# Top-k attention and MLP on one core: q/k loads ten steps later, and value copies moved behind the step's exponents

## The chip, the core and the metric

The kernel runs on one core of a Trainium2 chip. The metric is the device time of one execution in microseconds (us), here as a median over several runs. The engines are named as the profile names them: PE is TensorE (PEld its weight loads), DVE is VectorE, ACT is ScalarE, POOL is GpSimd, and SP is SyncE, which here issues every transfer. SPq is the SyncE queue's own work of issuing.

## The reference

Sparse attention is followed by a two-layer MLP. For 8 batches of 8 heads, 576 tokens and a head size of 64:

```python
scores = scale * np.matmul(q, k.transpose(0, 1, 3, 2))
kth = np.partition(scores, -top_k, axis=-1)[..., -top_k:-top_k + 1]   # top_k = 32
scores = np.where(scores >= kth, scores, -1000000000.0)
attn = np.exp(scores - np.max(scores, axis=-1, keepdims=True))
attn = attn / (np.sum(attn, axis=-1, keepdims=True) + 1e-09)
x = np.matmul(attn, v)                  # then heads side by side: 4608 tokens x 512
h = x @ w_in                            # 512 -> 2048
out = np.maximum(0.01 * h, h) @ w_out   # 2048 -> 512
```

So each row of scores keeps its 32 largest entries, and everything else gets a weight of zero.

## The kernel before

**Units and steps.** Two heads that lie side by side form a pair; there are 32 pairs, four to a batch. A unit is 128 query rows of one pair with both its heads (or the left-over 64 rows of two pairs), so a batch has 18 units, and there are 144 in all. The main loop walks over steps `s`, one unit a step. The order of every engine's instructions is the order in which this loop writes them (`manual_schedule`); no scheduler moves them. In step `s`:

- VectorE searches the 32 largest entries of unit `s` (`top_k`: four rounds of MAX8 at L249 and MATCH_REPLACE8 at L252, from the halves that L244 makes). A round is a `slot()`.
- GpSimd masks unit `s - 1` (`mask`, L262 and L263).
- ScalarE takes the exponents of unit `s - 1` (`exponents`, L266, first head in mid-step, second head at the end) and writes their sums (`sums`, `ze`, L271).
- Unit `s - 2` is normalized: reciprocals on VectorE (`rz`, L275), the product on ScalarE (L278). Then its weights are transposed: ScalarE splits the words into 16-bit halves (`split`, L287), SyncE writes them to DRAM (`apart`, L288) and reads them back with a transposing DMA (`wT`, L290). Units 15, 23 and 31 (`HURRIED`) are transposed on TensorE instead (L300), and ScalarE copies the result from PSUM (L306).
- Every second step TensorE computes the scores of the two units that begin two and three steps later (`scores`, L214), and ScalarE copies them out of PSUM (L221).
- Every second step TensorE weighs the values of two older units (`weigh_values`, L327), and ScalarE copies the result to `x` (`keep_values`, L341). For units 0 to 13 that stands in the middle of a step (`MIDDLE`), four steps after the later unit; afterwards at the end of a step (`END`), three steps after it, or two for a hurried unit.
- Between these, `mlp_steps` puts pieces of the MLP of token chunks that are ready: the first layer at L378 (at L352 for the first two chunks, with transposes at L362), its activation at L384, the second layer at L390, the copy and the store at L397 and L398. A chunk is ready when the values of all its units are in `x`.

**What sets the order around the change.** [...] A copy `x<-wide` on ScalarE waits for TensorE's L327, and whatever the step wrote behind it on ScalarE waits as well. A transfer issued by SyncE waits in the same way ahead of the writes and transposes that follow.

**Loads.** q and k of a pair (288 KB each, `load_qk`, L162 and L163) have eight places: five in the pool `loads`, three in the pool `raws`, which held the weights at first. v of a pair (320 KB, `load_v`, L168) has five. At the end of each step `load_more(s)` starts the loads whose place is free: those of q and k from the step on in which the scores of the place's last unit have been written, since `last[pair] - 2 <= s`; those of v four steps after that unit's own step. Two pairs come free in the same step in even batches.

**Before the loop** the weights of the MLP come as 64-bit words and are put together in single precision (L102 to L149), until about 75 us. At the end, when no unit is left, the rest of the MLP runs alone.

Of the kernel before, what the change touches and what calls it, by code (L numbers as in the profile page):

```python
# [19 lines left out]
def kernel(  # L20
# [35 lines left out]
    LOADED, LOADED_V = 5, 5  # L56
# [38 lines left out]
    def load_weights(n):  # L95
        if n >= NPIECE:
            return
        if not AS_WORDS:
            nc.sync.dma_start(piece(n), weights[n])
            return  # L100
        raw_of[n] = raws.tile([P, WCH, 4], U16, name="raw")
        nc.sync.dma_start(raw_of[n].rearrange("p n w -> p (n w)"), weights[n])  # L102
# [50 lines left out]
    qk_of, v_of = {}, {}  # L153

    def load_qk(pi):
        if pi % (LOADED + 3) < LOADED:
            qt = loads.tile([P, S], F32, name="qt")
            kt = loads.tile([P, S], F32, name="kt")
        else:
            raw = raws.tile([P, WCH, 4], U16, name="raw").rearrange("p n w -> p (n w)").bitcast(F32)  # L160
            qt, kt = raw[:, 0:S], raw[:, S:2 * S]
        nc.sync.dma_start(qt, qT[pi])  # L162
        nc.sync.dma_start(kt, kT[pi])  # L163
        qk_of[pi] = qt, kt

    def load_v(pi):
        v_of[pi] = loads.tile([P, NKC, 2, D], F32, name="vt", bufs=LOADED_V)
        nc.sync.dma_start(v_of[pi], vk[pi])  # L168
# [54 lines left out]
    def first_scores(u):  # L223

        ps = [ps_sc.tile([P, 2, 512], F32, name="wide", bufs=2) for i in range(2)]
        for half in range(2):
            for i, pi, side, r0 in u.parts:
                qt, kt = qk_of[pi]
                d = slice(side * D, (side + 1) * D)
                nc.tensor.matmul(ps[i][:, half, 0:HS], qt[d, u.q0:u.q0 + P],  # L230
                                 kt[d, half * HS:(half + 1) * HS], start=True, stop=True)
        u.both = work.tile([P, 2, S], F32, name="s_sb", bufs=5)
        u.s = [u.both[:, i, :] for i in range(2)]
        for i in range(2):
            nc.scalar.copy(u.s[i].rearrange("p (h n) -> p h n", h=2), ps[i][:, :, 0:HS])
# [33 lines left out]
    def sums(u):  # L269
        u.ze = small.tile([P, 2], F32, name="ze")  # L270
        nc.scalar.activation(u.ze, u.z, AF.Copy, bias=1e-9, scale=1.0)  # L271

    def reciprocals(u):
        u.rz = small.tile([P, 2], F32, name="rz")
        nc.vector.reciprocal(u.rz, u.ze)  # L275

    def normalize(u, i):
        nc.scalar.activation(u.s[i], u.s[i], AF.Copy, bias=0.0, scale=u.rz[:, i:i + 1])  # L278
# [33 lines left out]
    def x_at(token):  # L312

        c = 0
        while token >= CHUNKS[c]:
            token -= CHUNKS[c]
            c += 1
        return c, token

    def weigh_values(u, po):  # L320
        n = u.rows
        po = po.rearrange("p (o n) -> p o n", n=n)
        for o, (pi, r0, r1) in enumerate(u.outs):
            vt = v_of[pi]
            for c in range(NKC):
                for side, r in ((0, r0), (1, r1)):
                    nc.tensor.matmul(  # L327
                        po[side * D:(side + 1) * D, o, :],
                        vt[:, c, side, :],
                        u.wT[:, c + side * NKC if c + 1 < NKC else c, r:r + n],  # L330
                        start=(c == 0), stop=(c == NKC - 1),
                    )

    def keep_values(u, po):
        n = u.rows
        po = po.rearrange("p (o n) -> p o n", n=n)
        ch, col = x_at(u.b * S + u.q0)
        if ch not in x_of:
            x_of[ch] = [xpool.tile([P, CHMAX], F32, name=f"x{c}") for c in range(HP)]
        for o, (pi, _, _) in enumerate(u.outs):  # L340
            nc.scalar.copy(x_of[ch][pi % HP][:, col:col + n], po[:, o, :])  # L341
# [85 lines left out]
    LAG = 3  # L427
    HURRY = 20
    HURRIED = (15, 23, 31)
    UNHURRIED = 14  # L430
    MIDDLE, END = 0, 1

    def values_at(n):

        if n < UNHURRIED:
            return (n | 1) + LAG + 1, MIDDLE
        return (n | 1) + LAG - ((n | 1) in HURRIED), END
# [3 lines left out]
    def unit(n):  # L441
        return steps[n] if 0 <= n < len(steps) else None

    done_tokens, ready_at = [0] * len(CHUNKS), []
    for n, u in enumerate(steps):
        ch, _ = x_at(u.b * S + u.q0)
# [5 lines left out]
    def attended(*place):  # L452
        for at, ch in ready_at:
            if at == place:
                ready.append(ch)
                backlog[0] += mlp_cost(ch)

    def slot_budget(s):

        after = [at for (at, _), _ in ready_at if at >= s]  # L460
        until = after[0] if after else s
        if len(after) >= len(CHUNKS) - EARLY:
            return EARLY_SHARE
        return backlog[0] / ((until + 1 - s) * SLOTS)
# [4 lines left out]
    with tc.manual_schedule():  # L469
        last = {p: n for n, u in enumerate(steps) for p in u.pairs}  # L470

        def load_more(s):

            for of, load, n, lag in ((qk_of, load_qk, LOADED + 3, -2), (v_of, load_v, LOADED_V, LAG + 1)):
                while len(of) < NPAIR and (len(of) < n or last[len(of) - n] + lag <= s):
                    load(len(of))


        for n in range(3):
            load_weights(n)  # L480
        rounding = {}
        for n in range(NPIECE + 2):
            for i in (n, n - 1, n - 2) if AS_WORDS else ():
                if 0 <= i < NPIECE:
                    if i == n:
                        rounding[i] = round_weights(i)
                    next(rounding[i], None)
            load_weights(n + 3)
            if 6 <= n < 6 + HP:
                load_qk(n - 6)  # L490
            elif n == NPIECE - 3:
                first_scores(steps[0])
            elif n == NPIECE:
                first_scores(steps[1])
            if n == NPIECE - 1:
                load_v(0)
                load_v(1)

        def weights_of(u):
            reciprocals(u)  # L500
            normalize(u, 0)
            normalize(u, 1)

        def values(*place):
            due = [u for n, u in enumerate(steps) if values_at(n) == place]
            if due:
                po = ps_sc.tile([P, 2, 512], F32, name="wide", bufs=2)[:, 0, 0:2 * P]
                po = po.rearrange("p (u n) -> p u n", u=2)
            else:
                return  # L510
            for part in (weigh_values, keep_values):
                for n, u in enumerate(due):
                    part(u, po[:, n, :])
            attended(*place)

        for s in range(len(steps) + LAG + 1):
            cur, old, older, new = unit(s), unit(s - 1), unit(s - 2), ()
            if s % 2 == 0:
                new = [u for u in steps[s + 2:s + 4] if u]
            picks = top_k(cur) if cur else iter(())  # L520
            budget = slot_budget(s)

            def slot():
                next(picks, None)

            slot()
            if old:
                mask(old, 0)
                mask(old, 1)
            late = s < HURRY and not {s - 1, s - 2} & set(HURRIED)  # L530
            if older and not late:
                weights_of(older)
            mlp_steps(budget)
            values(s, MIDDLE)
            slot()
            if older and late:
                weights_of(older)
            if s - 2 in HURRIED:
                transpose_in_haste(older)
            mlp_steps(budget)  # L540
            if old:
                exponents(old, 0)
            if older:
                keep_transposed(older) if s - 2 in HURRIED else transpose(older)
            slot()
            mlp_steps(budget)
            mlp_steps(budget)
            slot()
            mlp_steps(budget)
            if old:  # L550
                exponents(old, 1)
                sums(old)
            if new and s < HURRY:
                scores(new)
            values(s, END)
            if new and s >= HURRY:
                scores(new)
            budget = slot_budget(s + 1)
            mlp_steps(budget)
            mlp_steps(budget)  # L560
            load_more(s)
        mlp_steps(1e9)

# [57 lines left out]
```

## Time and profile before

| | |
|---|---|
| time, median of 3 runs | 1487.02 us (1486.28 to 1489.58) |
| span of the profiled execution | 1484.5 us |
| TensorE busy | 1395.5 us, 94% |
| VectorE busy | 1328.7 us, 90% |
| ScalarE, GpSimd busy | 1095.9 and 1096.1 us, 74% each |
| moved by DMA | 223.48 MB, 53.5% of the DMA engines' span |
| transposes by DMA | 141, one for each unit that is not hurried |

The busy shares are averages over stages. The start (weights, first units) leaves TensorE idle for want of work; from about 260 us on it is busy in nearly every stretch. VectorE ends at about 1406 us, and TensorE works alone from there. Where a wait is given as "idle before, releaser", the releaser is the engine or transfer that came last.

### The profile page before, as it was taken

The page shows a single profiled execution, that of the slowest core. Times are in us where ns is not written, and L with a number is a line of the kernel's source. Part 1 is how long each engine was busy: PE and PEld are TensorE (multiplying, and loading weights), DVE is VectorE, ACT ScalarE, POOL GpSimd, SP SyncE. Part 2 cuts the span into 40 slices and gives each one's busy share as a digit, 9 for nine tenths or more (in the row PEclk, how much of TensorE's full clock was granted, in tenths as well). Part 3 has the DMA queues.
Part 4 walks back from the last instruction along what each step waited for, and adds up shares of the span by engine and source line. Part 5 has one row for each costly group of instructions (what it writes and reads, how often), then busy time and mean ns, then how long its engine had stood idle before and what let it go on. Part 6 is the DMA issues. An engine that isn't in the chain of part 4 may idle for free.

```text
span 1484.5 us, 24084 instructions
## 1 busy us (share of the span) xinstructions
PE 1395.5 (94%) x8059; PEld 929.4 (63%) x8059; DVE 1328.7 (90%) x3414; ACT 1095.9 (74%) x1979; POOL 1096.1 (74%) x742
## 2 busy tenths in 40 slices
PE   6715998999999999999999999999999999999998
PEld 2303546666666766676767666767676767676674
DVE  7999998999999999999999999999999999999600
ACT  8647786877788877787878777777777777877720
POOL 2278887888788887888878888888788888788700
PEclk9967998999999999999999999999999999999999
DMA  8824454645565465655664566555655555655510
GB/s 319 306 64 128 118 164 119 177 111 145 157 167 154 136 164 158 183 133 155 184 163 139 144 166 173 166 143 148 186 154 152 128 142 128 169 129 142 144 47 14
DMA packets 391420, 223.48 MB, mean 151 GB/s; under 512 B 336256, under 2 KB 336256, under 8 KB 389248
## 3 DMA queue, kind: packets, MB, share of 16 engines
q1 hardware_dynamic: 391296, 221.95, 53.5%
q8 instruction: 63, 1.03, 0.3%
q14 instruction: 61, 0.50, 0.1%
HBM read 46.14 MB, written 92.60 MB: 93 GB/s over the span
## 4 chain that ended last, share of the span: by engine, by line
PE 87%; DVE 7%; ACT 3%; DMA 2%; issue 1%; POOL 0%; DVEq 0%; SPq 0%; ACTq 0%
PE pz L390 33%; PE ph L378 31%; PE wide L327 11%; PE wide L214 6%; PE narrow L214 3%; DVE tops L249 2%; DVE pairs L252 1%; PE ph L352 1%; DMA wT<-apart 1%; ACT split L287 1%; DVE w_out L149 1%; DVE w_in L149 1%; DVE scale L146 1%; DVE pairs L244 1%; DMA apart<-split 1%; ACT s_sb L278 1%
## 5 line engine op out<-in xcount | busy, mean ns | idle before, releaser
L262 POOL TENSOR_SCALAR pen<-s_sb,tops 128x576 f32<-128x576 f32 x288 | 637.4, 2213 | 219.0 <-DVE tops L249 127.9
L249 DVE MAX8 tops<-pairs 128x8 f32<-128x288 f32 (+1 forms) x1152 | 636.5, 592 | 0.0
L390 PE MATMUL pz<-w_out,gT 128*128 128x512 f32 x1152 | 509.5, 597 | 0.0
L378 PE MATMUL ph<-x,w_in 128*128 128x256 f32 x2176 | 481.5, 381 | 0.0
L252 DVE MATCH_REPLACE8 pairs<-tops,pairs 128x288 f32<-128x288 f32 (+1 forms) x864 | 460.5, 539 | 0.0
L378 PEld LDWEIGHTS ph<-x,w_in 128*128 128x128 f32 x2176 | 411.1, 190 | 77.3 <-issue 23.1
L263 POOL TENSOR_TENSOR s_sb<-s_sb,pen 128x576 f32<-128x576 f32 x288 | 406.3, 1411 | 24.1
L390 PEld LDWEIGHTS pz<-w_out,gT 128*128 128x128 f32 x1152 | 215.9, 190 | 266.4 <-issue 265.0
L287 ACT COPY split<-s_sb 128x1152 uint16<-128x1152 uint16 x282 | 309.1, 1144 | 0.0
L278 ACT ACTIVATE s_sb<-s_sb,rz 128x576 f32<-128x576 f32 x288 | 207.0, 769 | 33.8 <-DVE rz L275 33.6
L266 ACT ACTIVATE s_sb<-s_sb,nbias 128x576 f32<-128x576 f32 x288 | 220.9, 767 | 12.7 <-POOL s_sb L263 12.7
L244 DVE TENSOR_TENSOR pairs<-s_sb 128x576 f32<-128x576 f32 x288 | 213.5, 780 | 9.9
L327 PE MATMUL wide<-wT,vt 128*64 128x128 f32 (+1 forms) x3200 | 181.1, 270 | 33.7 <-ACT s_sb L221 24.8
L327 PEld LDWEIGHTS wide<-wT,vt 128*64 128x64 f32 x3200 | 163.3, 140 | 76.6 <-ACT s_sb L221 29.4
L341 ACT COPY x<-wide 128x128 f32<-128x128 f32 (+1 forms) x160 | 32.2, 260 | 148.9 <-PE wide L327 148.8
L384 ACT ACTIVATE gT<-ph 128x512 f32<-128x512 f32 x136 | 80.6, 592 | 80.5 <-PE ph L378 80.5
L221 ACT COPY s_sb<-wide 128x704 f32<-128x704 f32 x142 | 107.1, 754 | 21.4 <-PE wide L214 21.3
L214 PE MATMUL wide<-kt,qt 64*128 64x352 f32 (+1 forms) x392 | 74.7, 491 | 24.3 <-ACT s_sb L221 23.6
L275 DVE RECIPROCAL rz<-ze 128x2 f32<-128x2 f32 x144 | 22.5, 156 | 54.4 <-ACT ze L271 54.1
L221 ACT COPY s_sb<-narrow 128x448 f32<-128x448 f32 x142 | 68.7, 536 | 0.7
L397 ACT COPY o_sb<-pz 128x512 f32<-128x512 f32 x36 | 21.1, 586 | 58.5 <-PE pz L390 58.5
L252 DVE MATCH_VALUE_LOAD pairs<-tops,pairs 128x8 f32 x864 | 63.2, 73 | 0.0
(62 smaller groups left out, 623.0 us busy)
## 6 DMA issues: line engine op xcount, KB each, us to landing
apart<-split SPq DMA_DIRECT2D x282, 288.0 KB, 2.1
raw<-in_weights_dram SPq DMA_DIRECT2D x16, 1024.0 KB, 6.9
vt<-in_vk_dram SPq DMA_DIRECT2D x32, 320.0 KB, 3.5
out_dram<-o_sb SPq DMA_DIRECT2D x36, 256.0 KB, 2.0
qt<-in_qT_dram SPq DMA_DIRECT2D x20, 288.0 KB, 4.4
kt<-in_kT_dram SPq DMA_DIRECT2D x20, 288.0 KB, 4.6
raw<-in_qT_dram SPq DMA_DIRECT2D x12, 288.0 KB, 3.6
raw<-in_kT_dram SPq DMA_DIRECT2D x12, 288.0 KB, 3.8
```

The source lines that it names most:

```text
L214: nc.tensor.matmul(to[r0:r0 + u.rows, i, :], qt[d, u.q0:u.q0 + u.rows], kt[d, k0:k1], start=True, stop=True)
L244: nc.vector.tensor_tensor(pairs[:, :, n, :], u.both[:, :, 0:HS], u.both[:, :, HS:S], op)
L249: nc.vector.max(out=u.tops[:, i, r, :], in_=rest[i])
L252: nc.vector.match_replace(out=rest[i], in_to_replace=u.tops[:, i, r, :], in_values=rest[i], imm_value=LOWEST)
L262: nc.gpsimd.tensor_scalar(pen, u.s[i], u.tops[:, i, ROUNDS - 1, 7:8], MASKED, ALU.is_lt, ALU.mult)
L263: nc.gpsimd.tensor_tensor(u.s[i], u.s[i], pen, ALU.add)
L266: nc.scalar.activation(u.s[i], u.s[i], AF.Exp, bias=u.nbias[:, i:i + 1], scale=SCALE, accum_out=u.z[:, i:i + 1])
L278: nc.scalar.activation(u.s[i], u.s[i], AF.Copy, bias=0.0, scale=u.rz[:, i:i + 1])
L287: nc.scalar.copy(split, pairs[:, :, h])
L327: nc.tensor.matmul(po[side * D:(side + 1) * D, o, :], vt[:, c, side, :], u.wT[:, c + side * NKC if c + 1 < NKC else c, r:r + n], start=(c ...
L378: nc.tensor.matmul(ph[:, i, 0:n], w_in[c][:, f * P:(f + 1) * P], x[c][:, 0:n], start=(c == 0), stop=(c == HP - 1),)
L390: nc.tensor.matmul(pz[0:m, 0:DMODEL], gT[:, f, r0:r0 + m], w_out[f // 4][:, f % 4, :], start=(f == 0), stop=(f == NFC - 1),)
```

## The change

There are two parts. The first is in `load_more`: v is looked at ahead of q and k; q and k are loaded from step `last[pair] + 8` on instead of `last[pair] - 2`; and apart from the first eight pairs only one pair is loaded a step. This takes the bursts of two pairs, which ran just when units were being transposed, apart, and moves them to places that have been free for long.

The second is in `values`: weighing and copying are two calls now. The copies of values weighed in mid-step stand behind the step's second exponents and its sums, so that these do not wait for TensorE. They stay where they were when a chunk becomes ready there, and in the steps two after a hurried unit (`at_once`). Copies at the end of a step stay.

```diff
-            for of, load, n, lag in ((qk_of, load_qk, LOADED + 3, -2), (v_of, load_v, LOADED_V, LAG + 1)):
+            for of, load, n, lag in ((v_of, load_v, LOADED_V, LAG + 1), (qk_of, load_qk, LOADED + 3, 8)):
                 while len(of) < NPAIR and (len(of) < n or last[len(of) - n] + lag <= s):
                     load(len(of))
+                    if lag > LAG + 1 and len(of) > n:
+                        break
...
-                return
-            for part in (weigh_values, keep_values):
-                for n, u in enumerate(due):
-                    part(u, po[:, n, :])
+                return ()
+            for n, u in enumerate(due):
+                weigh_values(u, po[:, n, :])
+            return [(u, po[:, n, :]) for n, u in enumerate(due)]
+
+        def keep(weighed, *place):
+            for u, po in weighed:
+                keep_values(u, po)
             attended(*place)
...
-            values(s, MIDDLE)
+            weighed = values(s, MIDDLE)
+            at_once = s - 2 in HURRIED or any(at == (s, MIDDLE) for at, _ in ready_at)
+            if at_once:
+                keep(weighed, s, MIDDLE)
...
                 exponents(old, 1)
                 sums(old)
+            if not at_once:
+                keep(weighed, s, MIDDLE)
             if new and s < HURRY:
                 scores(new)
-            values(s, END)
+            keep(values(s, END), s, END)
```

## The prediction

> **What bounds the kernel now.** I read the page first (engine shares and the chain that ended last), then the waits of TensorE, then busy time by stage, then the order of time around each place where TensorE stood still.
>
> ```profile
> PE 1395.5 (94%) x8059; PEld 929.4 (63%) x8059; DVE 1328.7 (90%) x3414; ACT 1095.9 (74%) x1979; POOL 1096.1 (74%) x742
> PE 87%; DVE 7%; ACT 3%; DMA 2%; issue 1%; POOL 0%; DVEq 0%; SPq 0%; ACTq 0%
> ```
>
> TensorE carries 87% of the chain, so the end comes when its fixed list of matmuls is done: only its idle time can be won. By stage (columns: stretch, length, busy us and instructions of PE, PEld, DVE, ACT, POOL, granted clock, DMA share, GB/s):
>
> ```profile
> 205.00:231.00 26.00, 25.21 (x189) 13.71 (x189) 22.52 (x62) 20.13 (x41) 19.52 (x14) 1.00 0.66 193
> 231.00:242.00 11.00, 4.90 (x41) 4.60 (x42) 10.90 (x29) 2.42 (x7) 8.94 (x7) 0.55 0.33 81
> 242.00:260.00 18.00, 18.00 (x89) 15.10 (x89) 12.86 (x33) 13.50 (x24) 11.48 (x8) 0.99 0.27 76
> 408.00:558.00 150.00, 147.49 (x865) 100.25 (x865) 148.73 (x388) 121.25 (x221) 126.25 (x86) 1.00 0.59 156
> 558.00:1397.00 839.00, 839.00 (x5058) 577.14 (x5055) 802.06 (x2089) 659.82 (x1215) 678.27 (x454) 1.00 0.57 153
> ```
>
> From 205 us on TensorE works without a break, but for one hole at 231 to 242 us (at a clock of 0.55) and 2.5 us between 408 and 558. After 558 it is full to the end of the attention, and then works off the MLP alone. So the question is what the change does to the hole, to the 2.5 us, and whether it opens new holes. The hole and the stalls before it, in order of time (start, length, engine, line, tiles; in brackets the idle time before):
>
> ```profile
> 213.71 0.43 ACT L341 COPY x<-wide 128x128 f32<-128x128 f32 x2 [4.34 <-PE wide L327]
> 219.36 0.17 DVE L275 RECIPROCAL rz<-ze 128x2 f32<-128x2 f32 x1 [3.34 <-ACT ze L271]
> 224.54 2.69 SPq L163 DMA_DIRECT2D kt<-in_kT_dram  x1
> 226.39 2.40 PE L327 MATMUL wide<-wT,vt 128*64 128x128 f32 x40
> 227.33 0.85 SPq L288 DMA_DIRECT2D apart<-split  x2
> 232.25 2.59 SPq L290 DMA_TRANSPOSE wT<-apart  x1
> 237.10 4.53 PE L327 MATMUL wide<-wT,vt 128*64 128x128 f32 x40 [6.41 <-DMA wT<-apart]
> 241.56 7.59 PE L378 MATMUL ph<-x,w_in 128*128 128x256 f32 x32
> 252.02 0.17 DVE L275 RECIPROCAL rz<-ze 128x2 f32<-128x2 f32 x1 [4.41 <-ACT ze L271]
> ```
>
> The matmuls at 237.10 are the values of units 14 and 15 (end of step 17). Unit 15 is transposed on TensorE; unit 14's weights come by DMA. Its second split ended at 223.86 on ScalarE, but the SyncE queue was still at a q/k load until 227.23, and so issued the writes at 227.33. The writes then shared the DMA engines with those loads: 4.92 us from write to transpose, where undisturbed units take 3.2 us. The same pattern in step 52:
>
> ```profile
> 547.58 1.27 SPq L288 DMA_DIRECT2D apart<-split  x2
> 552.99 2.72 SPq L290 DMA_TRANSPOSE wT<-apart  x1
> 557.79 1.31 PE L327 MATMUL wide<-wT,vt 128*64 128x128 f32 x20 [1.65 <-DMA wT<-apart]
> ```
>
> Two pairs of q/k were issued at 544.75 to 547.54; 5.41 us instead of 3.2; TensorE waits 1.65 us.
>
> [...] after 6.41 us idle the 40 matmuls took 4.53 us, against 2.40 us at 226.39, with a granted clock of 0.55. [...] 2.69 us for one load's issue at 224.54 against 0.43 us for the one ahead of it, and the writes right behind.
>
> **Part 1, the copies.** Values are weighed in mid-step only for units 0 to 13 (steps 5, 7, 9, ..., 17). Steps 7 and 11 complete an MLP chunk, and step 17 belongs to a hurried unit; these stay as they were. Copies move in steps 5, 9, 13, 15 alone, and TensorE's order does not change at all. ScalarE's waits for TensorE at those copies were 2.92, 1.64, 1.75 and 4.34 us; the normalization, exponents, split and sum of the step stood behind.
> - Step 5: VectorE is not idle there, so nothing is gained: its next reciprocals come on time.
> - Step 9: VectorE waits 0.84 us at 163.52 for the sum of step 9. That goes: 0.8 us for VectorE, and TensorE, which is fed by ScalarE until its last small wait at 204.94, follows. I count 0.8 us (0 to 1.4, as a 0.56 us wait at 181.91 comes from step 11, which is unchanged, and may or may not persist).
> - Step 13: no VectorE wait follows; ScalarE merely gains 2.2 us of slack. Zero.
> - Step 15: without the copies ScalarE starts normalizing at 209.37 (end of the score copies) in place of 214.03. Adding 1.44, 0.96, 2.19, 0.96 and 0.2 us from the same rows, the sum ze is out at about 215.1 instead of 219.33. VectorE is ready at 216.02, so its 3.34 us vanish, and unit 14's split in step 16 moves from 223.86 to about 220.8. The copies then run at 215, when TensorE has long finished (213.66). The PSUM buffer they hold longer is needed next by the scores at 222.37: no wait.
>
> **Part 2, the loads.** Pairs 8 to 11 left at 209 to 227 us (steps 14 and 15); they now leave one a step in steps 24 to 27, and later batches likewise. Bytes and counts are unchanged. For the hole: unit 14's first write can go at about 219.8, its transpose at 219.8 + 3.2 = 223.0, and with the transpose's 4.6 us to landing the weights are there at 227.7. TensorE comes to them at 230.7, as before, after the transposes of unit 15 (which it reaches by its own unbroken work from 205). So the DMA no longer ends the wait. What ends it is ScalarE's copy of unit 15's transposed weights out of PSUM, which also frees the buffer the values need: 230.3 + 1.0 = about 231.3 us. The values start at 231.3 instead of 237.10: 5.8 us. The idle time is then about 1 us, so I expect no clock drop: 4.53 - 2.40 = 2.1 us more, and 7.59 - 7.0 = 0.5 us for the 32 matmuls behind (the row at 1.00 clock takes 14.01 for 64).
>
> Can the rest keep up? VectorE loses its 3.34 us and also the 4.41 us at 252.02, because ScalarE no longer sits 8.28 us at the value copies of 241.67, waiting for TensorE. With 0.8 that is 8.6 us against TensorE's 9.2: the next values (units 16, 17) had their second weights landing at 266.6, just when TensorE reached them; both move by about the same amount. Step 52: the loads are gone from its write, so 1.65 us go. The 0.86 us wait at 413.57 is not tied to loads; I count 0.4 for the shift in alignment.
>
> Cost of the new places: one pair of q/k (0.59 MB) ahead of a write. Batches of before already have it: at 703.28 a single pair 1.1 us ahead of a write made it 5.00 us, at 694.54, 2.7 us ahead, 3.20 us; neither stopped TensorE. The second unit of a couple has only 0 to 1.7 us of slack between landing and use (I compared landings with the value matmuls from 265 to 640 us; zero at 338, in step 28, right behind the new loads). Between 0 and 1.8 us for a couple there; I take 1.0 us in all. Need for the data: pair 8 arrives in step 24 and is first used in step 34. The values' loads ahead of q/k at step 0 go out at 53 to 66 us, before the first write at 95.13: nothing.
>
> Sum: 0.8 + 5.8 + 2.1 + 0.5 + 1.65 + 0.4 - 1.0 = 10.3 us; 1487.0 - 10.3 = 1476.7 us.
>
> **Rivals.** (a) The hole closes, but VectorE and ScalarE do not follow: TensorE waits again at units 16/17, 24/25 and 32/33, where slack is about zero, and gives half back. For: those three zero slacks. Against: VectorE's waits are themselves waits on TensorE through ScalarE. About 5 us gained: 1482. (b) The deadline merely moves: no DMA wait, but as long a wait on ScalarE or VectorE in step 17, and new loads eat the rest: 1486 to 1488, no change. Against: at 230.85 ScalarE was already copying unit 15's weights. (c) Slower: single loads stretch the transposes in four steps of each of six batches. If in each batch two couples lose 1.7 us beyond their slack, that costs 20 us against 10.3: 1497. Against: the single pairs at 694 to 723 stopped nobody.
>
> **How the numbers follow.** Forecast (8 to 13 us gained) 0.65; (a) 0.23; (b) 0.07; (c) 0.05. The low end takes every bound in favour (1.4 early, no loss at new loads, the whole 0.86: 12.4 us, and a little for VectorE's other waits of 1.86 and 2.82 us): 1473. The high end takes in most of (a): 1482.5. Faster by over 0.2% (3 us): the forecast and nearly all of (a), 0.87; same 0.08; slower 0.05.
>
> **What would show it.** Right: no wait over 1.5 us before the values of units 14 and 15, that group at 2.4 us for 40, about 231 us; granted clock near 1.00 at 231 to 242; no reciprocal waits of 3.34 and 4.41 us; write to transpose about 3.2 us in steps 16 and 52. Wrong: the values of step 17 still at 237, or TensorE waits for weights at steps 24 to 29, 40 to 45 or later which add up to more than 3 us.

## The result, and the profile after

The changed kernel takes 1476.05 us (median of 4 runs, 1474.74 to 1476.92) against 1486.65 us for the kernel before beside it (1486.08 to 1489.58): 10.6 us or 0.76% faster, ratio 0.9924 with a 95% interval of 0.9907 to 0.9941. A second measurement gave 1476.14 us and 0.9924 (0.9911 to 0.9938). The prediction was 1476.7 us.

From the page of the changed kernel, the shares of the engines and the chain that ended last:

```profile
PE 1393.5 (95%) x8057; PEld 927.6 (63%) x8059; DVE 1328.3 (90%) x3414; ACT 1096.2 (74%) x1979; POOL 1097.7 (74%) x742
PE 81%; DVE 14%; DMA 2%; ACT 2%; issue 1%; SPq 0%; POOL 0%; DVEq 0%; ACTq 0%
```

The work of the engines is what it was; the span of the profiled execution fell from 1484.5 to 1473.8 us. VectorE has 14% of the chain in place of 7%, which may mean that TensorE now reaches some places just when VectorE does; no run tests that. Busy time of the changed kernel by the same stages (columns as in the prediction):

```profile
205.00:231.00 26.00, 24.93 (x193) 14.07 (x187) 25.76 (x68) 20.18 (x40) 21.97 (x15) 0.98 0.46 124
231.00:242.00 11.00, 11.00 (x75) 8.97 (x72) 10.54 (x30) 6.46 (x12) 9.53 (x7) 1.00 0.12 44
408.00:558.00 150.00, 150.00 (x878) 102.73 (x877) 148.59 (x389) 121.55 (x221) 126.43 (x85) 1.00 0.60 163
```

The hole at 231 to 242 us is gone: TensorE is busy for all 11.00 us, at a clock of 1.00 in place of 0.55. VectorE is busy for 25.76 of 26 us before it, where it had 22.52. TensorE is full from 408 to 558 us as well, where it stood still for 2.5 us; a wait of 0.94 us is left just ahead of that stage, at 403.99. In order of time, the changed kernel around step 17:

```profile
212.69 0.42 ACT L341 COPY x<-wide 128x128 f32<-128x128 f32 x2
215.62 2.19 ACT L287 COPY split<-s_sb 128x1152 uint16<-128x1152 uint16 x2
216.78 1.39 SPq L288 DMA_DIRECT2D apart<-split  x2
219.99 2.46 SPq L290 DMA_TRANSPOSE wT<-apart  x1
229.87 2.40 PE L327 MATMUL wide<-wT,vt 128*64 128x128 f32 x40 [1.07 <-ACT wT L306]
232.21 7.17 PE L378 MATMUL ph<-x,w_in 128*128 128x256 f32 x32
242.26 0.17 DVE L275 RECIPROCAL rz<-ze 128x2 f32<-128x2 f32 x1 [0.68 <-ACT ze L271]
```

The copy of step 15 no longer waits, unit 14's split runs at 215.62 to 217.81 instead of ending at 223.86, its write needs 3.21 us to the transpose, and the values of step 17 start at 229.87 instead of 237.10. They wait 1.07 us, for ScalarE's copy of unit 15's transposed weights, and take 2.40 us instead of 4.53. VectorE's wait of 3.34 us is gone and that of 4.41 is 0.68.

Where the time came from is best seen by following TensorE: its instructions have the same order in both kernels, so I subtract the start of the same group of value matmuls. The table gives how many us earlier TensorE is than in the kernel before, at eight places, named by their time in the kernel before; "changed, again" is the profile of the second measurement:

```
kernel            115.6   190.7   226.4   237.1   265.2   554.8   575.1   1405.1
changed            0.90    3.67    1.12    7.23    9.77    9.58   11.45    10.75
changed, again     0.79    3.40    0.97    7.08    9.62    9.23   11.11    11.34
```

The 0.9 us at the start are not the change's: they are there while the MLP weights are still being loaded, ahead of the first instruction that differs. Over all kernels below this lead lies between -0.04 and 1.02 us. Nearly everything else comes in two places: the hole (6.1 us at 237.1, and 2.5 us right behind it from the full clock), and step 52 (1.9 us at 575.1).

### The profile page after: what moved, and what is told of

Its sections match the earlier page's. It is cut to its first block, busy times and chain, and to the rows that moved or that the text cites. A ratio compares the mean times of both kernels' runs of the same rounds, so it can differ in the third digit from the quotient of the medians.

```text
span 1473.8 us, 24093 instructions
## 1 busy us (share of the span) xinstructions
PE 1393.5 (95%) x8057; PEld 927.6 (63%) x8059; DVE 1328.3 (90%) x3414; ACT 1096.2 (74%) x1979; POOL 1097.7 (74%) x742
## 4 chain that ended last, share of the span: by engine, by line
PE 81%; DVE 14%; DMA 2%; ACT 2%; issue 1%; SPq 0%; POOL 0%; DVEq 0%; ACTq 0%
PE pz L390 31%; PE ph L378 30%; PE wide L327 10%; PE wide L214 6%; DVE tops L249 5%; DVE pairs L252 4%; PE narrow L214 3%; DVE pairs L244 1%; DMA wT<-apart 1%; ACT split L287 1%; DVE w_out L149 1%; DVE w_in L149 1%; DVE scale L146 1%; DVE scale L124 0%; ACT s_sb L278 0%
```

## The experiments

Ratios are to the kernel before on the same chip, with their 95% intervals. The same subtraction for all of them:

```
kernel            115.6   190.7   226.4   237.1   265.2   554.8   575.1   1405.1
loads alone        0.76   -0.51   -2.20    1.58    4.12    3.25    5.12     5.09
copies alone      -0.04    3.43   -0.40    5.71    8.25    8.15    7.75     7.50
soon, one a step   0.29    2.69    0.51    6.62    9.16    9.12   10.99    10.63
late, in twos      1.02    3.79    1.25    7.35    9.89   10.08   11.95    11.03
only step 15       0.18    0.62    0.62    6.72    9.26    8.37   10.25     9.41
all but step 15    0.29    2.70    0.52    4.38    6.92    6.50    8.38     8.64
share 510          1.01    3.71    1.01    6.89    9.43    8.93   10.81    10.93
share 600          0.11   -3.69   -4.65   -0.42    2.12    0.95    2.83     3.13
share 700          0.93  -10.17   -4.26    0.09    2.63    1.58    3.46     3.49
```

**Each part alone.** The new `load_more` in the kernel before, and the old `load_more` in the changed kernel:

```diff
-            for of, load, n, lag in ((qk_of, load_qk, LOADED + 3, -2), (v_of, load_v, LOADED_V, LAG + 1)):
+            for of, load, n, lag in ((v_of, load_v, LOADED_V, LAG + 1), (qk_of, load_qk, LOADED + 3, 8)):
                 ...
+                    if lag > LAG + 1 and len(of) > n:
+                        break
```

> The new load places with the value copies where they were before. Theory A (either part alone closes most of the hole, since TensorE's own work is what ends last without the loads): unit 14's split still ends near 223.9 us after the same start, its write goes at about 222.9, the transpose follows after 3.2 us instead of 4.92, the values of step 17 start at about 232 us instead of 237.1 and take 2.4 us for 40; VectorE still waits 3.3 us for the sum of step 15, and TensorE waits up to 2 us for units 16 and 17. Sum 5.2 + 2.6 + 1.65 + 0.4 - 1.0 - 1.0: about 1479 us (1477.5 to 1481). Theory B (the parts add: the copies carry about half of the 10.6 us): 1481 to 1483 us, with a wait of 3 us or more left before the values of step 17. Theory C (the loads do it all, the copies nothing): 1476 to 1477 us.

> The moved copies with the loads where they were before. Theory A (either part alone closes most of the hole): the split of unit 14 ends 3 us earlier, the loads of two pairs also go earlier but still stand ahead of its write, which then takes about 5 us to its transpose; the values of step 17 wait 1 to 3 us for the weights and start at 231 to 233 us; the 1.65 us wait in step 52 stays. About 1479 us (1477.5 to 1481). Theory B (the parts add): about 1481 us. Theory C (the loads do it all): within 2 us of the kernel before, 1485 to 1487 us.

Measured: loads alone 1481.01 us, 0.9955 (0.9941 to 0.9969); copies alone 1478.77 us, 0.9942 (0.9929 to 0.9955). The hole in loads alone:

```profile
215.91 0.43 ACT L341 COPY x<-wide 128x128 f32<-128x128 f32 x2 [5.20 <-PE wide L327]
222.69 2.47 SPq L290 DMA_TRANSPOSE wT<-apart  x1
225.21 1.20 SPq L288 DMA_DIRECT2D apart<-split  x2
230.66 2.61 SPq L290 DMA_TRANSPOSE wT<-apart  x1
235.52 2.40 PE L327 MATMUL wide<-wT,vt 128*64 128x128 f32 x40 [2.64 <-DMA wT<-apart]
```

and in copies alone:

```profile
219.24 0.43 SPq L163 DMA_DIRECT2D kt<-in_kT_dram  x1
219.77 0.85 SPq L288 DMA_DIRECT2D apart<-split  x2
225.30 2.70 SPq L290 DMA_TRANSPOSE wT<-apart  x1
231.39 2.40 PE L327 MATMUL wide<-wT,vt 128*64 128x128 f32 x40 [1.07 <-ACT wT L306]
```

With the loads alone, the wait for weights shrinks from 6.41 to 2.64 us and no further. The write is no longer held by the queue: the first half of the split ends at about 225.0, and the write goes at 225.21. Yet it takes 5.45 us to its transpose, with no load of q, k or v anywhere near. What does lie there is a transfer that no line of the kernel issues. The DMA view of a stretch lists it as `instruction`: one packet of 16 KB, at 226.70 to 228.31 in loads alone. Here are its line for 225.2 to 231 us, the row of a late part of the same write (its DMA share is the last but one number), and the only line for the same write in the changed kernel, 216.8 to 220 us:

```profile
q8 instruction: 1, 0.02, 1.7%
228.40:229.80 1.40, 1.40 (x23) 1.22 (x24) 1.40 (x5) 1.29 (x3) 1.32 (x2) 1.00 0.06 20
q1 hardware_dynamic: 1420, 0.87, 88.5%
```

From 228.4 us on the DMA engines are busy for 0.06 of the time, as much as one of the 16 that the page counts. That this one is the engine which had the 16 KB is my reading; no view here names it. In the changed kernel the write has landed by 219.91, ahead of the transfer of this kind at 223.81. As an estimate, without it the write of loads alone would take 3.4 us (the mean of 101 writes in these profiles that stood as close behind a transpose with no load and no such transfer beside them), and the weights would land at about 233.3. ScalarE's copy L306, which starts at 233.04 there, would then end the wait at about 234.1 (in the changed kernel the values start 1.06 us after it), and 1.4 of the 2.64 us would go.

With the copies alone, two pairs of q/k still stand ahead of the write and it takes 5.53 us, but everything is so much earlier that no wait for weights is left: the remaining 1.07 us are the same as in the changed kernel. So theory C falls (the loads don't do it all), and B falls for the hole: the copies alone close all of it, the loads alone over half. On top of the moved copies the loads bring what lies in step 52. The value matmuls there in copies alone, and then in the changed kernel:

```profile
545.11 2.85 SPq L290 DMA_TRANSPOSE wT<-apart  x1
550.04 1.31 PE L327 MATMUL wide<-wT,vt 128*64 128x128 f32 x20 [2.05 <-DMA wT<-apart]
```

```profile
537.88 1.39 SPq L288 DMA_DIRECT2D apart<-split  x2
541.10 2.77 SPq L290 DMA_TRANSPOSE wT<-apart  x1
545.24 2.40 PE L327 MATMUL wide<-wT,vt 128*64 128x128 f32 x40
```

In copies alone the write had gone at 539.49, right behind two pairs of q/k and 5.62 us ahead of its transpose, and TensorE waits 2.05 us: it loses 0.4 us between 554.8 and 575.1. With the loads moved as well the same write takes 3.22 us, the 40 matmuls run without a break, and TensorE gains 1.87 us there. The two parts overlap: less the lead at the start, 7.5 us for the copies and 4.3 for the loads, but 9.9 together. The figure for the loads is a low one: TensorE ran at a granted clock of 0.5 for 3.41 us from 206.31 us on in that profile (last section), and the 16 KB fell on the write.

**Later, or one a step?** The loads changed in two ways at once. So each was taken alone: once `lag` back at -2, but with one pair a step (the first eight pairs free of the limit, as in the changed kernel); once `lag` at +8, without the limit:

```diff
-... (qk_of, load_qk, LOADED + 3, 8)):
+... (qk_of, load_qk, LOADED + 3, -2)):
-                    if lag > LAG + 1 and len(of) > n:
+                    if lag < 0 and len(of) > n:
```
```diff
-                    if lag > LAG + 1 and len(of) > n:
-                        break
```

> The changed kernel, but loads of q and k from the step on in which they were before (last - 2), one pair a step. Theory A (with the copies moved there are some 3 us of slack, and one pair ahead of a write costs at most 1.8 us): no wait over 1.5 us before the values of step 17 or in step 52; 1476 to 1478 us. Rival (lateness is what counts, loads at -2 meet the writes in the steps without slack): a wait for transposed weights of 1.5 us or more in step 17 or 52, and 1478.5 us or more.

> The changed kernel without the limit of one pair a step: loads of q and k ten steps later, two pairs a step where two come free. Theory A (only steps 14 to 17 and 50 to 52 had no slack, so that where the loads go is what matters): 1476 to 1478 us, with no new wait over 1 us. Rival (two pairs together stretch a write to 5 us wherever they meet one, and steps 24 to 28 have no slack): a wait of 1.5 to 2.5 us for weights near the values of units 24 and 25, and 1478 to 1480 us.

Measured: soon, one a step 1475.34 us, 0.9918 (0.9904 to 0.9931); late, in twos 1475.77 us, 0.9921 (0.9908 to 0.9935). Both have the whole gain, 10.3 and 10.0 us less the lead at the start (9.9 for the changed kernel), and neither waits for weights in step 17 or 52. Late in twos waits 0.6 us once for a load of v and 0.8 us for weights near step 36; nothing appears near units 24 and 25. With the copies moved, either half of the change of loads is enough; both rivals fall.

**Which copies.** Only step 15's moved; and all but step 15's:

```diff
-            at_once = s - 2 in HURRIED or any(at == (s, MIDDLE) for at, _ in ready_at)
+            at_once = s != 15
```
```diff
+            at_once = s == 15 or s - 2 in HURRIED or any(at == (s, MIDDLE) for at, _ in ready_at)
```

> The changed kernel, but of the four moved copies only those of step 15 are moved; steps 5, 9 and 13 have them where they were before. Theory A (the copies of step 15 alone hold back the split of unit 14, and what steps 9 and 13 give TensorE is given back before 205 us): no wait for transposed weights in step 17, only the 1.1 us for ScalarE's copy; VectorE's waits of 0.84 and 0.56 us near 163 and 182 us are back; 1475 to 1477.5 us. Rival (the early steps carry the 1.7 us that VectorE gained by step 15): 1478 to 1479 us.

> The changed kernel, but the copies of step 15 stand where they were before; those of steps 5, 9 and 13 are moved. Theory A (step 15 is what counts): like the new load places alone, a wait of 2 to 3 us for transposed weights before the values of step 17 and a VectorE wait of 3 us for the sum of step 15; 1479 to 1482 us. Rival (the early steps do it): 1476 to 1478 us.

Measured: only step 15 1477.98 us, 0.9929 (0.9916 to 0.9941); all but step 15 1478.87 us, 0.9933 (0.9921 to 0.9946). The medians lie close, and neither is in the range of theory A or of its rival; the profiles differ most in step 17. With only step 15 the values of step 17 wait 1.07 us for ScalarE and nothing for weights; less the lead, 9.2 of 9.9 us are there. Without step 15:

```profile
213.19 0.43 ACT L341 COPY x<-wide 128x128 f32<-128x128 f32 x2 [5.38 <-PE wide L327]
218.84 0.17 DVE L275 RECIPROCAL rz<-ze 128x2 f32<-128x2 f32 x1 [4.85 <-ACT ze L271]
222.47 1.22 SPq L288 DMA_DIRECT2D apart<-split  x2
227.97 2.51 SPq L290 DMA_TRANSPOSE wT<-apart  x1
232.72 2.40 PE L327 MATMUL wide<-wT,vt 128*64 128x128 f32 x40 [2.56 <-ACT s_sb L266]
```

The picture of loads alone is back: the copies held for 5.38 us, 5.50 us from write to transpose (with 16 KB of kind `instruction` at 224.00 to 225.65, and again a DMA share of 0.06 behind it), 2.56 us of waiting. The releaser named, ScalarE's exponents, had long been done; the weights land then (the transpose was issued at 227.97, and the median from issue to landing is 4.6 us on the page of the kernel before).

So step 15 is the copy that decides the wait for weights, as theory A has it. It is not the only copy worth moving. Without it 8.4 us of the gain are still there (8.64 less 0.29), 4 us more than with the loads alone; by the medians, 1478.87 against 1481.01 us. TensorE is already 3.2 us further ahead of loads alone at 226.4, of which up to 1.7 us are the low clock of that one profile (an estimate: half of its 3.41 us). On top of step 15 the early steps bring only 0.6 us (9.9 against 9.2). Like copies and loads, the two groups of copies overlap.

**TensorE's own order before step 17.** `EARLY_SHARE` is the budget of a slot while only the first two chunks of the MLP are there; I changed it to 600, 700 and 510:

```diff
-    EARLY_SHARE = 500
+    EARLY_SHARE = 600
```

> The changed kernel with EARLY_SHARE 600 in place of 500: TensorE takes more of the first two chunks' MLP in each slot up to step 14, and has less of it left between 205 and 230 us. Theory A (after the change TensorE's own list sets when the values of step 17 start): the 3.9 us wait near 200 us shrinks, the values of step 17 start 1 to 3.5 us earlier, 1472.5 to 1475 us. Rival (VectorE and ScalarE bound step 17 already, or idle time ahead of it lets the clock fall): the values of step 17 not earlier, or 4 us long for 40; 1476 to 1479 us.

> The same with EARLY_SHARE 700. Theory A: no more gain than with 600, since the reciprocals of unit 15 (222 us) and its transposes then bound the values of step 17 at about 226.5 us and TensorE idles ahead of them; 1473 to 1477 us. Rival (all of TensorE's work before 230 us counts, the more of it early the better): another 1 to 2 us below share 600.

> The changed kernel with EARLY_SHARE 510: in step 14 ScalarE's activation L357 now stands ahead of the split of unit 12, and one step of two matmuls moves ahead of the scores; nothing else of weight moves. Theory A (the wait of 3.9 us near 200 us and the low clock after it are what the moved copies of steps 9 and 13 lost again; a small shift of the order takes them away): the wait falls below 2 us, the scores of step 14 run at full clock, the values of step 17 start 1 to 3 us earlier; 1473 to 1475.5 us. Rival (as with 600: whatever TensorE does ahead of the scores of step 14 holds ScalarE, which holds step 17): the values of step 17 later, 1476 to 1480 us.

Measured: 1482.5 us, 0.9961 (0.9948 to 0.9975); 1482.53 us, 0.9963 (0.9951 to 0.9976); 1476.16 us, 0.9924 (0.9911 to 0.9936), with the changed kernel at 1476.14 beside the last. The expectations failed: 600 and 700 are slower than theory and rival had it, and 510 brings nothing. With 600 the wait of 3.9 us near 200 us does go (1.99 us for `gT` are left), but the rows of ScalarE and of TensorE show what came for it:

```profile
199.81 12.26 PE L390 MATMUL pz<-w_out,gT 128*128 128x512 f32 x24 [1.99 <-ACT gT L363]
212.89 0.75 ACT L221 COPY s_sb<-wide 128x704 f32<-128x704 f32 x1 [6.12 <-PE wide L214]
231.04 4.27 PE L327 MATMUL wide<-wT,vt 128*64 128x128 f32 x40 [4.39 <-ACT s_sb L221]
```

Twelve matmuls of the second layer (24 instructions) now stand ahead of the scores of step 14. ScalarE waits 6.12 us for these scores with the normalization and exponents of step 15 behind, units 12 and 13 come late, and TensorE waits 4.39 us and then takes 4.27 us for 40 matmuls that take 2.40 in the changed kernel. With 510 the wait of 3.9 us shrinks to 1.0, but 2.7 us of waiting for `gT` take its place. The first eight score matmuls of step 14 take 0.82 us, as in the kernel before at a granted clock of 1.00, and not 1.45 as in the changed kernel; the low clock falls on the four matmuls of the second layer ahead of them instead (3.68 us, where four take 1.98 later; granted clock 0.50 at 202.6 to 205.9). The values of step 17 start 6.9 us earlier than before, as in the changed kernel. None of these versions is clearly faster than the changed kernel.

## Why the prediction was right, and where not

The sum was right, 10.3 predicted and 9.9 us in the profile less the lead at the start (10.6 by the medians). Term by term:

- **Bound.** That only TensorE's idle time after 205 us counts held: the gain of the changed kernel sits in the hole and in step 52, and of the 2.8 us that TensorE was further ahead at 190.7 all but 0.2 were lost again by 226.4.
- **Early steps, 0.8.** Measured 0.2 (1.12 less 0.90 at 226.4). VectorE's two small waits at 163.52 and 181.91 did go, and TensorE was 2.8 us further ahead at 190.7. It then ran into a longer wait for ScalarE's L357, 3.92 us for 2.01, and behind it into a granted clock of 0.50 from 202.51 to 205.92 us, where the kernel before had 1.00 from 203 to 210. The changed kernel, then the kernel before:

```profile
202.19 0.85 PE L362 MATMUL pt<-ident,scale 128*128 128x128 f32 x4 [3.92 <-ACT scale L357]
202.97 1.45 PE L214 MATMUL wide<-kt,qt 64*64 64x352 f32 x8
```

```profile
204.94 0.66 PE L362 MATMUL pt<-ident,scale 128*128 128x128 f32 x4 [2.01 <-ACT scale L357]
205.53 0.82 PE L214 MATMUL wide<-kt,qt 64*64 64x352 f32 x8
```

- **The hole, 5.8.** Measured 6.1 (7.23 less 1.12), ended by ScalarE's copy L306 as predicted. The working put these 5.8 us under the loads, and that attribution is what failed: the copies of step 15 suffice for it, and the loads alone leave 2.64 us. So the sum came out in spite of its split between the two parts. Two readings under it fared differently. That a write is slower right behind loads stands: the writes of 4.92 and 5.41 us in the kernel before, issued at 227.33 and 547.58, have no `instruction` transfer beside them, and the loads ahead of them were still under way (they landed at 228.61 to 230.77 and at 549.34 to 551.49 us). But the 2.69 us for which the queue was held at one load were read as the load's own. Counted after 100 us in the twelve profiles, 851 issues of loads with no such transfer in their first 0.6 us took at most 0.58 us, also as the fourth in a row, and every one of the 19 over 0.9 us had one there; this load had 16 KB at 224.61 to 226.86. So the load stood in the way, but it was long only, as far as the traces show, where it met such a transfer: at 0.43 us the write would have gone 2.3 us earlier (an estimate).
- **Clock, 2.1 + 0.5.** Measured 2.5 (9.77 less 7.23): 40 matmuls took 4.53 us after 6.41 us of waiting, with a granted clock of 0.55 at 231 to 242 us, and 2.40 us after 1.07 us of waiting in the changed kernel, with 1.00. That about 1 us would bring no low clock was an estimate of mine. How long a wait may be is not shown: in loads alone the clock was low after 2.00 us, in the kernel before it was not after 2.01 (last section).
- **VectorE keeps up.** Right: rival (a) would have given half back at units 16 to 33; the lead stays at 9.77 to 9.58 from 265 to 555 us.
- **Step 52, 1.65.** Measured 1.87. **Step 36, 0.4.** Measured none: a wait of 0.94 us stays, where the kernel before had 0.86.
- **New places, -1.0.** -0.2 us up to 555, and -0.7 from 575 to 1405 us (11.45 to 10.75), which the second measurement doesn't show (11.11 to 11.34). Nothing near rival (c).
- **Small slips in its sums.** The bounds of the low end add up to 12.3 us, not 12.4; 7.59 less 7.0 is 0.6, not 0.5; and 3.34 us off 223.86 is 220.5, not 220.8. Nothing hangs on them.

## What to carry to other kernels

A copy that waits for a far-ahead engine should stand behind whatever feeds the next stage of its own engine; look for the step in which the chain of transfers behind it has no slack, since there one blocked copy costs a wait two steps later (2.56 us here, with the copies of step 15 where they were). When one write or one issue takes far longer than its like (here 5.45 us against a mean of 3.25, and 2.69 against 0.43), see what else was on the DMA engines in that stretch, transfers that the program does not issue included, before it is put down to its neighbours. Two remedies for one hole are not worth their sum: run each alone before one is credited. And before moving more work forward to fill a small gap, see which engine will then wait for what it displaces (here ScalarE, 6.12 us).

## What was not expected of the hardware

Transfers of kind `instruction`, of which the profiles of the kernel before and of the changed kernel show 124 each of 8 or 16 KB, go with most of the odd times here. I took the first write of every unit after 100 us in the twelve profiles, and split them by whether such a transfer ran in the 3.2 us after the issue, and whether a load lay between the two transposes around the write. Us from the write to its transpose:

```
                                                        writes   mean   most   over 4.3 us
no load, no instruction transfer                           855   3.25   3.82             0
no load, instruction transfer                              328   3.83   5.65            78
only writes 3 to 4 us behind the transpose before:
    load, no instruction transfer                          139   4.85   7.07
    no load, no instruction transfer                       189   3.24   3.78
```

From 6 to 7 us behind the transpose the mean is 3.23 us with a load or without one (66 and 92 writes, no instruction transfer). So the writes with a load close ahead took longer (4.85 against 3.24 us on average), and so did those with an instruction transfer (3.83 against 3.25). Without either, 101 writes only 2 to 2.6 us behind a transpose still took 3.41 us. That the two cause the long times is read from this sorting and from the DMA share of 0.06 above; no run moved an instruction transfer alone. Transposes show the same: of 730 with such a transfer in the 4.3 us after their issue 178 took over 5.5 us to land, of 950 without one a single one did. One of them did no harm: in the changed kernel it comes at 223.81, on the transpose of unit 14, which takes 6.13 us to land, at 226.1, and the values that need it start at 229.87.

The low clock does not follow the wait alone: after 2.01 us of waiting the eight score matmuls took 0.82 us in the kernel before, at a granted clock of 1.00, and after 2.00 us 1.23 us in loads alone, where the granted clock was 0.5 for 3.41 us from 206.31 on. At half the clock for 3.41 us, that is up to 1.7 us at that one place (an estimate); whether other executions of that kernel have it is not shown.
